# Weight sums moved to GpSimd in the third dense stage, and fraction bits to ScalarE in the last one

## The chip, the cores and the metric

One core of a Trainium2 chip runs the kernel: TensorE (matmuls), VectorE, ScalarE, GpSimd and the DMA queues, each with an in-order queue of its own. The metric is the time of one execution on the device in microseconds; of several runs the median counts.

## The reference, cut to what matters

Attention with a capped score feeds two feed-forward blocks. All dense weights arrive as 64-bit floats.

```
x = attention(q, k, v, cap)          # 2 x 12 heads, 448 tokens, 64 wide -> 896 x 768
h = x @ w_in1;  g = h * cos(h);      y = g @ w_out1     # 768 -> 2048 -> 768
h = y @ w_in2;  g = h * sigmoid(h);  out = g @ w_out2   # 768 -> 2048 -> 768
```

## The kernel before

**Stages.** The attention goes over twelve pairs of heads. Four dense stages follow: `gemm_in` (w_in1 and the cosine), `gemm_out` (w_out1), `gemm_sums` (w_in2 and the silu) and `gemm_last` (w_out2). Each engine works through its instructions in the order in which the program issues them; that order is written out by hand.

**Weights.** A block of 128 x 768 weights comes by DMA into `wraw` (two buffers) as pairs of 32-bit words, low word first. `w_abs` (line 135, ScalarE) turns the high word without its sign into a number with the exponent of a 32-bit float. `w_bits` then runs three VectorE operations, called conversions below: line 146 keeps the sign, line 148 shifts and adds the sign, line 151 adds the top three bits of the low word, the last three fraction bits. A pair of blocks has six conversions. The 32-bit result lies in `wx`. For the matmuls it is split into a high part, a rounded copy by ScalarE (`w_hi`, `take`, lines 159 and 709), and a low part, the difference, by VectorE (`w_lo`, `low`, lines 166 and 713); three matmuls (high x high, high x low, low x high) make a product exact enough.

**Third dense stage.** `gemm_sums` computes two output blocks from two weight blocks (a pair) and both batches by seven products M1 to M7 instead of eight, with sums of weight blocks. A product is nine matmuls. There are eight pairs, p = 0 to 7. The sums lie in one tile, `sums` in the trace: `s31` (line 689, 768 elements per partition) gives S31 and `s24` (lines 693 and 694, 384 each, the second from the first) gives S24. `A` and `A22` are blocks of the weights themselves. While TensorE works on pair p, the generator `weights(p+1)` issues the work on the next pair in seven portions: first block's conversions; second block's; `take` A and `s31`; `low` A and `take` S31; `s24` and `low` S31; `take` and `low` of S24; `take` and `low` of A22. Portions and products alternate. `copy` (line 789, ScalarE), `add` (line 761, VectorE) and `silu` (line 756, ScalarE) read the banks of the products:

```
m1(p)                      # bank A[p % 3]
c12(p - 1)                 # an add, line 761
next(w); m5_(p); next(w)   # the six conversions of pair p + 1
m7(p - 1)                  # add(p - 1 + HP, A[(p - 1) % 3], ...), line 761
next(w); m2(p); next(w); m6(p); next(w); next(w)
m4(p - 1)                  # goes on adding into bank A[(p - 1) % 3]
next(w); m3(p)
```

So `m4(p-1)` may start only when the `add` of `m7(p-1)` has read the bank, and that `add` is issued after the six conversions of pair p+1. In the round p = 1 there is no `m7(p-1)`, and `m4(0)` stands in its place.

**Last stage.** `gemm_last` has two halves of the output columns with eight weight blocks each and seven groups of 128 tokens; a weight block takes 42 matmuls. `last_w` prepares block n three blocks ahead: load, conversions, `w_hi`, `w_lo`, `w_abs` of the next. `g_split` (lines 934 and 935) splits the activations of the blocks p and p+8 in the same way, two rounds ahead.

Of the kernel before, what the change touches and what calls it, by code (L numbers as in the profile page):

```python
# [29 lines left out]
F32R = mybir.dt.float32r  # L30
I32 = mybir.dt.int32
U32 = mybir.dt.uint32
AF = mybir.ActivationFunctionType
ALU = mybir.AluOpType
PSUM = bass.MemoryType.PSUM
# [2 lines left out]
def tile_attention_ffn_ffn(  # L38
# [10 lines left out]
    nc = tc.nc  # L49
# [13 lines left out]
    HK = KD // 2  # L63
# [35 lines left out]
    wjobs = []  # L99
    for w_in, w_out in ((w_in1, w_out1), (w_in2, w_out2)):  # L100
        wi, wo = w_in.bitcast(I32), w_out.bitcast(I32)
        for n in range(KF):
            fc = n if w_out is w_out1 else n // 2 + n % 2 * HP
            wjobs.append((KD, wi[fc]))
        if w_out is w_out1:
            for dm in range(KD):
                for k0, k1 in cuts:
                    wjobs.append((k1 - k0, wo[dm][:, 2 * P * k0:2 * P * k1]))
        else:
            for half in range(DM // DH):  # L110
                for k0 in range(0, KF, KO):
                    wjobs.append((KO * DH // P, wo[half][:, 2 * DH * k0:2 * DH * (k0 + KO)]))
    wraw, w32, wlo, whi, loaded, guarded = {}, {}, {}, {}, set(), set()
    wx = wpool.tile([P, 2, KMAX, P], I32, name="wx")
    room = [wpool.tile([P, KMAX, P], F32R, name=f"hl{n}") for n in range(2 * NW)]
# [13 lines left out]
    def w_abs(i, t=None):  # L129
        if i not in wraw or i in guarded:  # L130
            return
        n = wjobs[i][0]
        guarded.add(i)
        w32[i] = wx[:, i % 2] if t is None else t
        nc.scalar.activation(out=w32[i][:, :n, :].bitcast(F32), in_=wraw[i][:, :n, :, 1].bitcast(F32), func=AF.Abs, scale=2.0 ** -112)  # L135

    def w_bits(i, step):
        if i >= len(wjobs):
            return
        n = wjobs[i][0]  # L140
        w1, w0 = wraw[i][:, :n, :, 1], wraw[i][:, :n, :, 0]
        if step == 0:
            w_abs(i)
        t = w32[i][:, :n, :]
        if step == 0:
            nc.vector.tensor_scalar(out=w1, in0=w1, scalar1=-0x80000000, scalar2=None, op0=ALU.bitwise_and)  # L146
        elif step == 1:
            nc.vector.scalar_tensor_tensor(out=t, in0=t, scalar=3, in1=w1, op0=ALU.logical_shift_left, op1=ALU.bitwise_or)  # L148
        else:
            t = t.bitcast(U32)  # L150
            nc.vector.scalar_tensor_tensor(out=t, in0=w0.bitcast(U32), scalar=29, in1=t, op0=ALU.logical_shift_right, op1=ALU.bitwise_or)  # L151
            del wraw[i]

    def w_hi(i):
# [3 lines left out]
        whi[i] = room.pop(0)  # L158
        nc.scalar.activation(out=whi[i][:, :n, :], in_=w32[i][:, :n, :].bitcast(F32), func=AF.Copy)  # L159

# [12 lines left out]
    with ExitStack() as actx:  # L173
# [19 lines left out]
        def v_init():  # L193
            nc.gpsimd.memset(ones[:, :2 * Q], 1.0)
            nc.gpsimd.memset(ones[:, 2 * Q:], 0.0)
# [53 lines left out]
        def S_tanh(p, t):  # L249
# [4 lines left out]
            n = 2 if t < 3 else 1  # L254
            nc.scalar.activation(out=e32[p][:, 2 * t:2 * t + n, :], in_=sc.pop((p, t))[:, :n, :S], func=AF.Tanh, scale=scap)  # L255

        def S_exp(p, chunks=slice(0, NCH)):
            if p >= NPT:
                return
            e = e32[p][:, chunks, :]  # L260
            nc.scalar.activation(out=e, in_=e, func=AF.Exp, scale=capt)  # L261

# [91 lines left out]
        for w, turn in ((0, 1), (1, 4), (2, 6)):  # L354
            for at, *step in ((0, w_abs, w), (1, w_bits, w, 0), (2, w_bits, w, 1), (3, w_bits, w, 2),
                              (3, w_load, w + 2, nc.gpsimd), (4, w_hi, w), (5, w_lo, w)):
                early.setdefault(turn + at, []).append(step)
        early.setdefault(NPT - 2, []).append((w_abs, 3))

        load(0)  # L360
        nc.vector.memset(zero.bitcast(F32), 0.0)
        warm_up(8, ps_o.tile([P, 512], F32, tag="sm", name="warm0")[:, :S])

        nc.scalar.activation(out=scap, in_=zero[:, :1].bitcast(F32), func=AF.Tanh)
        v_init()
# [128 lines left out]
    def w_do(f, ws, *a):  # L494
        for wi in ws:
            f(wi, *a)
# [5 lines left out]
    def cos_unit(pieces, ws):  # L502
        pieces = cut(pieces)
        for h, r, gh, gl in pieces:
            nc.scalar.activation(out=r.bitcast(I32), in_=h, func=AF.Copy, scale=1.0 / (2.0 * math.pi))
        w_do(w_bits, ws, 0)
        for h, r, gh, gl in pieces:
            nc.vector.scalar_tensor_tensor(out=r, in0=h, scalar=1.0 / (2.0 * math.pi), in1=r.bitcast(I32),
                                           op0=ALU.mult, op1=ALU.subtract)
        for h, r, gh, gl in pieces:  # L510
            nc.scalar.activation(out=r, in_=r, func=AF.Sin, scale=math.pi)
        w_next(ws)
        for h, r, gh, gl in pieces:
            nc.scalar.activation(out=r, in_=r, func=AF.Square)
        w_do(w_bits, ws, 1)
        w_do(w_bits, ws, 2)
        w_do(w_hi, ws)
        rest()
        for h, r, gh, gl in pieces:
            nc.vector.scalar_tensor_tensor(out=r, in0=r, scalar=-0.5, in1=h, op0=ALU.add, op1=ALU.mult)  # L520
        w_do(w_lo, ws)
        for h, r, gh, gl in pieces:
            nc.scalar.activation(out=gh, in_=r, func=AF.Copy)
            left.append((r, gh, gl))
# [142 lines left out]
    blocks, whole, xw = {}, {}, {0: wx}  # L667
# [18 lines left out]

    def s31(p):
        x = xw[p % 2].bitcast(F32)
        nc.vector.tensor_tensor(out=xw["s"][:, 0:2], in0=x[:, :, :HK, :], in1=x[:, 1].rearrange("p (n k) f -> p n k f", n=2), op=ALU.subtract)

    def s24(p):
        x, s = xw[p % 2].bitcast(F32), xw["s"]
        nc.vector.tensor_tensor(out=s[:, 2], in0=x[:, 0, :HK], in1=s[:, 1], op=ALU.subtract)
        nc.vector.tensor_tensor(out=s[:, 3], in0=x[:, 0, HK:], in1=s[:, 2], op=ALU.subtract)

    def source(p, what):
        x, s = xw[p % 2].bitcast(F32), xw["s"]
# [20 lines left out]
    def first_pair(n):  # L718
        if n == 0:
            w_half(0, 0)  # L720
        elif n == 1:
            s31(0)
            take(0, "A")
            low(0, "A")
            take(0, "S31")
            s24(0)
            low(0, "S31")
        else:
            take(0, "S24")
            low(0, "S24")  # L730
            take(0, "A22")
            low(0, "A22")
# [15 lines left out]
    def gemm_sums(pt0):  # L748
# [49 lines left out]
        def weights(q):  # L798
            w_load(base_s + 2 * q + 1)
            w_half(q, 0)  # L800
            w_load(base_s + 2 * q + 2)
            w_abs(base_s + 2 * q + 1, xw[q % 2][:, 1])
            yield
            w_half(q, 1)
            w_load(base_s + 2 * q + 3)
            yield
            take(q, "A")
            s31(q)
            yield
            low(q, "A")  # L810
            take(q, "S31")
            yield
            s24(q)
            low(q, "S31")
            yield
            take(q, "S24")
            low(q, "S24")
            yield
            take(q, "A22")
            low(q, "A22")  # L820
            abs_pair(q + 1)
            yield
# [237 lines left out]
```

## Time and profile before

| what | value |
|---|---|
| median of 3 runs | 551.69 us (551.6 to 552.08) |
| profiled execution | 551.79 us, of it 550.0 us span |
| granted TensorE clock, mean | 0.999 |
| TensorE busy | 542.1 us, 99% of the span |
| VectorE busy | 404.9 us, 74% |
| ScalarE busy | 309.0 us, 56% |
| GpSimd busy | 31.1 us, 6% |
| third dense stage, 327.29 to 429.44 us | VectorE 88.55 us busy, ScalarE 63.51, GpSimd 0 |
| last stage, 429.44 to 545.94 us | VectorE 64.56 us busy, ScalarE 38.15, GpSimd 0 |

The span is the stretch from the first to the last recorded instruction; the profiled execution's own time is somewhat longer. Busy time is work in the engine, not proof that the engine sets the end: the chain that ended last and the waits tell that.

### The profile page before, as it was taken

To read this page: it belongs to the slowest core of one execution; us is meant where nothing else is said; L and a number is where in the kernel's file an instruction comes from. 1 tells how busy PE (TensorE), PEld (TensorE's weight loads), DVE (VectorE), ACT (ScalarE), POOL (GpSimd) and SP (SyncE) were. 2 spreads that over 40 slices of the span, in tenths; PEclk is the share of its full clock that TensorE was granted. 3 is DMA by queue.
4 is the path that set the end of the run, shared out by engine and by line. 5 is a ranking of instruction groups with operands and counts; after the bars stand their busy time and mean duration, and the time that the engine had idled before them with its cause. 6 is when DMAs were issued, how large, how long until landed. Compare 5 with 4: busy or idle time off the path is not lost.

```text
span 550.0 us, 7421 instructions
## 1 busy us (share of the span) xinstructions
PE 542.1 (99%) x2940; PEld 467.2 (85%) x2940; DVE 404.9 (74%) x556; ACT 309.0 (56%) x393; POOL 31.1 (6%) x50
## 2 busy tenths in 40 slices
PE   8999999999999999999999999999999999999997
PEld 5444443999999999999999999999999999999996
DVE  4479997699888888666447888999886789537401
ACT  6989995477777665452323356566665556223101
POOL 0244432000000000000000000000000000000000
PEclk9999999999999999999999999999999999999999
DMA  7156652143322333452223603444331335164002
GB/s 291 55 141 199 171 166 78 44 142 120 109 94 102 115 95 106 153 154 88 72 99 103 217 8 114 147 160 153 116 114 58 116 116 172 58 215 144 30 1 101
DMA packets 17191, 65.13 MB, mean 118 GB/s; under 512 B 3384, under 2 KB 7268, under 8 KB 17156
## 3 DMA queue, kind: packets, MB, share of 16 engines
q1 hardware_dynamic: 14096, 54.94, 30.8%
q0 software_dynamic: 2496, 9.18, 5.4%
q10 hardware_dynamic: 564, 0.54, 0.3%
q8 instruction: 23, 0.38, 0.3%
q14 instruction: 12, 0.10, 0.1%
HBM read 61.74 MB, written 2.80 MB: 117 GB/s over the span
## 4 chain that ended last, share of the span: by engine, by line
PE 95%; ACT 2%; issue 1%; DMA 1%; DVE 1%
PE bank L473 21%; PE ps L473 21%; PE bank L967 21%; PE bank L741 19%; PE po L277 5%; PE sc L243 3%; PE sm L295 2%; PE sc L247 2%; PE po L287 2%; ACT e L255 1%; DMA raw<-in_qkv 1%; ACT e L261 1%; DVE e L303 0%; DVE ql L227 0%; DVE qh L226 0%
## 5 line engine op out<-in xcount | busy, mean ns | idle before, releaser
L473 PE MATMUL ps<-x,hl 128*128 128x448 f32 x576 | 117.0, 365 | 0.0
L473 PEld LDWEIGHTS ps<-x,hl 128*128 128x128 f32 x576 | 108.1, 188 | 9.2 <-DVE xs L314 0.7
L473 PE MATMUL bank<-gh,hl 128*128 128x448 f32 x288 | 83.9, 366 | 0.0
L159 ACT ACTIVATE hl<-wx 128x768 fp32r<-128x768 f32 (+1 forms) x44 | 35.8, 814 | 64.3 <-DVE wx L151 61.5
L967 PE MATMUL bank<-hl,gsh 128*128 128x384 f32 x280 | 71.0, 334 | 0.0
L151 DVE SCALAR_TENSOR_TENSOR wx<-wraw,wx 128x768 uint32<-128x768 uint32 (+1 forms) x66 | 61.6, 934 | 2.2
L148 DVE SCALAR_TENSOR_TENSOR wx<-wx,wraw 128x768 int32<-128x768 int32 (+1 forms) x66 | 61.5, 932 | 1.6
L135 ACT ACTIVATE wx<-wraw 128x768 f32<-128x768 f32 (+1 forms) x66 | 57.9, 877 | 6.3 <-DMA wraw<-in_moe_w_out 3.5
L473 PEld LDWEIGHTS bank<-gh,hl 128*128 128x128 f32 x288 | 54.1, 188 | 4.4
L166 DVE TENSOR_TENSOR hl<-wx,hl 128x768 fp32r<-128x768 f32 (+1 forms) x44 | 40.4, 918 | 20.4 <-ACT hl L159 20.3
L473 PE MATMUL bank<-gl,hl 128*128 128x448 f32 x144 | 52.6, 365 | 0.0
L967 PEld LDWEIGHTS bank<-hl,gsh 128*128 128x128 f32 x280 | 50.5, 188 | 0.0
L741 PE MATMUL bank<-T,hl 128*128 128x448 f32 x234 | 50.2, 365 | 0.0
L741 PEld LDWEIGHTS bank<-T,hl 128*128 128x128 f32 x234 | 43.9, 188 | 3.5
L967 PE MATMUL bank<-hl,gsl 128*128 128x384 f32 x140 | 46.8, 334 | 0.0
L255 ACT ACTIVATE e<-sc,scap 128x896 f32<-128x896 f32 (+1 forms) x48 | 40.0, 911 | 6.5 <-PE sc L243 6.5
L146 DVE TENSOR_SCALAR wraw<-wraw 128x768 int32<-128x768 int32 (+1 forms) x66 | 36.0, 546 | 5.1 <-ACT wx L135 4.9
L261 ACT ACTIVATE e<-e,capt 128x3136 f32<-128x3136 f32 (+2 forms) x13 | 35.2, 2710 | 0.4
L473 PE MATMUL bank<-g,hl 128*128 128x448 f32 x144 | 31.2, 365 | 0.0
L1000 DVE COPY os<-bank 128x384 f32<-128x384 f32 x6 | 3.3, 557 | 36.4 <-PE bank L967 36.4
L277 PE MATMUL po<-e,vf 128*64 128x448 f32 x144 | 29.4, 540 | 0.7 <-ACT e L261 0.7
L473 PEld LDWEIGHTS bank<-g,hl 128*128 128x128 f32 x144 | 27.1, 188 | 2.2
(107 smaller groups left out, 820.7 us busy)
## 6 DMA issues: line engine op xcount, KB each, us to landing
wraw<-in_moe_w_in SPq DMA_DIRECT2D x29, 768.0 KB, 4.2
wraw<-in_moe_w_out SPq DMA_DIRECT2D x22, 768.0 KB, 4.3
wraw<-in_moe_w_out SPq DMA_DIRECT2D x12, 640.0 KB, 4.1
raw<-in_qkv POOLq DMA_DIRECT2D x9, 480.0 KB, 4.6
out<-os SPq DMA_DIRECT2D x13, 192.0 KB, 1.9
rb<-rs SPq DMA_DIRECT2D x22, 112.0 KB, 3.3
wraw<-in_moe_w_in POOLq DMA_DIRECT2D x3, 768.0 KB, 6.4
vf<-in_qkv POOLq DMA_DIRECT2D x10, 224.0 KB, 4.6
```

The source lines that it names most:

```text
L135: nc.scalar.activation(out=w32[i][:, :n, :].bitcast(F32), in_=wraw[i][:, :n, :, 1].bitcast(F32), func=AF.Abs, scale=2.0 ** -112)
L146: nc.vector.tensor_scalar(out=w1, in0=w1, scalar1=-0x80000000, scalar2=None, op0=ALU.bitwise_and)
L148: nc.vector.scalar_tensor_tensor(out=t, in0=t, scalar=3, in1=w1, op0=ALU.logical_shift_left, op1=ALU.bitwise_or)
L151: nc.vector.scalar_tensor_tensor(out=t, in0=w0.bitcast(U32), scalar=29, in1=t, op0=ALU.logical_shift_right, op1=ALU.bitwise_or)
L159: nc.scalar.activation(out=whi[i][:, :n, :], in_=w32[i][:, :n, :].bitcast(F32), func=AF.Copy)
L166: nc.vector.tensor_tensor(out=wlo[i][:, :n, :], in0=w32.pop(i)[:, :n, :].bitcast(F32), in1=whi[i][:, :n, :].bitcast(F32), op=ALU.subtract)
L255: nc.scalar.activation(out=e32[p][:, 2 * t:2 * t + n, :], in_=sc.pop((p, t))[:, :n, :S], func=AF.Tanh, scale=scap)
L261: nc.scalar.activation(out=e, in_=e, func=AF.Exp, scale=capt)
L277: nc.tensor.matmul(po[u * D:(u + 1) * D], vf[p][:, 2 * t + u, :], e32[p][:, 2 * t + u, :], start=first and n == 0, stop=last and n == len( ...
L473: nc.tensor.matmul(pt, l, r, start=first and m == 0, stop=last and m == len(ops) - 1)
L741: nc.tensor.matmul(bank, x, y, start=first and m == 0, stop=m == len(ops) - 1, skip_group_check=True)
L967: nc.tensor.matmul(pt[t], a, r[:, cols], start=p == 0 and x == 0 and m == 0, stop=p == HP - 1 and x == 1 and m == 2)
```

## The change

Two edits. In the third dense stage the sums `s31` and `s24` are issued on GpSimd instead of VectorE for the pairs p = 2 to 7. In the last stage, for the last thirteen of its sixteen weight blocks, ScalarE reads the top byte of each low word, scales and shifts it so that the conversion to a whole number leaves its top three bits, and writes that whole number back as the low word, right behind `w_abs`. VectorE's three operations become two: the sign joined with the low word, then the shift joined with the result.

```
+    BYTES = len(wjobs) - 13
@@ w_abs
+        if i >= BYTES:
+            b = wraw[i][:, :n].rearrange("p k f t -> p (k f) t")
+            nc.scalar.activation(out=b[:, :, 0], in_=b.bitcast(U8)[:, :, 3], func=AF.Copy, scale=1.0 / 32, bias=-0.5 + 1.0 / 64)
@@ w_bits
-        if step == 0:
+        if i >= BYTES:
+            if step == 1:
+                nc.vector.scalar_tensor_tensor(out=w1, in0=w1, scalar=-0x80000000, in1=w0, op0=ALU.bitwise_and, op1=ALU.bitwise_or)
+            elif step == 2:
+                nc.vector.scalar_tensor_tensor(out=t, in0=t, scalar=3, in1=w1, op0=ALU.logical_shift_left, op1=ALU.bitwise_or)
+                del wraw[i]
+        elif step == 0:
@@ s31
-        nc.vector.tensor_tensor(out=xw["s"][:, 0:2], in0=x[:, :, :HK, :], in1=x[:, 1].rearrange("p (n k) f -> p n k f", n=2), op=ALU.subtract)
+        eng = nc.gpsimd if p > 1 else nc.vector
+        eng.tensor_tensor(out=xw["s"][:, 0:2], in0=x[:, :, :HK, :], in1=x[:, 1].rearrange("p (n k) f -> p n k f", n=2), op=ALU.subtract)
@@ s24
-        nc.vector.tensor_tensor(out=s[:, 2], in0=x[:, 0, :HK], in1=s[:, 1], op=ALU.subtract)
-        nc.vector.tensor_tensor(out=s[:, 3], in0=x[:, 0, HK:], in1=s[:, 2], op=ALU.subtract)
+        eng = nc.gpsimd if p > 1 else nc.vector
+        eng.tensor_tensor(out=s[:, 2], in0=x[:, 0, :HK], in1=s[:, 1], op=ALU.subtract)
+        eng.tensor_tensor(out=s[:, 3], in0=x[:, 0, HK:], in1=s[:, 2], op=ALU.subtract)
```

## Rows read from the trace of the kernel before

**Rows 1.** The page's chain that ended last, by engine.

```profile
PE 95%; ACT 2%; issue 1%; DMA 1%; DVE 1%
```

**Rows 2.** The same chain in order of time: start us, us, what.

```profile
327.29 102.15 PE bank L741 x504
429.44 116.50 PE bank L967 x672
```

**Rows 3.** Timeline of ScalarE, end of the last stage: start us, us, instruction, [idle before].

```profile
539.72 0.49 ACT L998 ACTIVATE os<-bank 128x384 f32<-128x384 f32 x1 [23.82 <-PE bank L967]
541.80 0.49 ACT L998 ACTIVATE os<-bank 128x384 f32<-128x384 f32 x1 [1.59 <-PE bank L967]
```

**Rows 4.** Timeline of VectorE, pair 2 of the third stage and what follows.

```profile
345.67 0.96 DVE L151 SCALAR_TENSOR_TENSOR wx<-wraw,wx 128x768 uint32<-128x768 uint32 x1
346.66 0.96 DVE L689 TENSOR_TENSOR sums<-wx 128x768 f32<-128x768 f32 x1
347.54 0.95 DVE L713 TENSOR_TENSOR hlx<-wx,hlx 128x768 fp32r<-128x768 f32 x1
348.41 0.55 DVE L693 TENSOR_TENSOR sums<-wx,sums 128x384 f32<-128x384 f32 x1
348.99 0.56 DVE L694 TENSOR_TENSOR sums<-wx,sums 128x384 f32<-128x384 f32 x1
...
352.34 0.55 DVE L146 TENSOR_SCALAR wraw<-wraw 128x768 int32<-128x768 int32 x1
...
357.26 0.62 DVE L761 TENSOR_TENSOR gf<-bank,m 128x448 f32<-128x448 f32 x1
...
369.05 0.62 DVE L761 TENSOR_TENSOR gf<-bank,m 128x448 f32<-128x448 f32 x1
```

**Rows 5.** Timeline of ScalarE in the same stretch.

```profile
347.65 0.85 ACT L709 ACTIVATE hl<-sums 128x768 fp32r<-128x768 f32 x1 [1.54 <-DVE sums L689]
...
357.91 0.58 ACT L756 ACTIVATE gf<-gf 128x448 f32<-128x448 f32 x1 [3.60 <-DVE gf L761]
358.40 0.83 ACT L709 ACTIVATE hl<-wx 128x768 fp32r<-128x768 f32 x1
```

**Rows 6.** Timeline of TensorE in the same stretch, neighbours of one kind merged.

```profile
350.84 3.81 PE L741 MATMUL bank<-T,hl 128*128 128x448 f32 x18
...
358.14 1.98 PE L741 MATMUL bank<-T,hl 128*128 128x448 f32 x9
```

**Rows 7.** Groups by line, GpSimd: count, busy us, mean ns of one, idle before.

```profile
L194 POOL MEMSET ones<- 128x64 f32 x1 | 0.2, 151 | 0.3 <-POOLq L1020 0.3
L195 POOL MEMSET ones<- 128x32 f32 x1 | 0.1, 125 | 0.0
```

**Rows 8.** Timeline of GpSimd in the attention stage, two stretches.

```profile
26.05 1.73 POOL L316 DMA_DIRECT2D sums<-xs  x2 [5.21 <-DVE sums L322]
...
28.35 0.93 POOL L215 DMA_DIRECT2D vf<-in_qkv  x1
...
82.34 1.22 POOL L316 DMA_DIRECT2D sums<-xs  x2 [2.21 <-DVE sums L322]
```

**Rows 9.** Timeline of VectorE in the same stretches.

```profile
27.06 0.57 DVE L226 CAST qh<-raw 128x832 fp32r<-128x832 f32 x1
...
28.60 0.56 DVE L146 TENSOR_SCALAR wraw<-wraw 128x768 int32<-128x768 int32 x1
...
82.41 1.02 DVE L303 TENSOR_TENSOR e<-e 128x896 f32<-128x896 f32 x1
```

**Rows 10.** Groups by line, ScalarE, last stage alone.

```profile
L135 ACT ACTIVATE wx<-wraw 128x768 f32<-128x768 f32 x14 | 12.5, 893 | 3.5 <-DMA wraw<-in_moe_w_out 3.5
```

**Rows 11.** Timeline of VectorE, first round of the last stage.

```profile
436.85 2.09 DVE L935 TENSOR_TENSOR gsl<-gf,gsh 128x896 fp32r<-128x896 f32 x2 [0.68 <-ACT gsh L934]
```

**Rows 12.** Timeline of TensorE, third round of the last stage.

```profile
443.84 0.51 PE L967 MATMUL bank<-hlx,gsh 128*128 128x384 f32 x2
```

More of the change, by code (lines that the diff above doesn't have):

```diff
@@ L32 @@
 U32 = mybir.dt.uint32
+U8 = mybir.dt.uint8
 AF = mybir.ActivationFunctionType
```

## The prediction

> **What bounds the kernel now.** I read the chain that ended last first, then its pieces in order of time, then the waits, then the timelines around the two edits. TensorE holds 95% of the chain [rows 1]. The third dense stage is one unbroken piece: 504 matmuls in 102.15 us, 202.7 ns each; the last stage is another: 672 in 116.50 us, 173.4 ns each [rows 2]. The waits name nobody for TensorE in either. So there is nothing to win in them unless a matmul itself gets cheaper when VectorE works less. Late in the last stage, with the weights done and VectorE idle, 12 matmuls still lie between two evacuations 2.08 us apart, 173.3 ns each [rows 3]: the same. The edits can move work about under a bound engine; the question is whether they uncover it.
>
> They could. The thinnest cover of the third stage is seen by following one pair through the queues. While TensorE multiplies pair p, VectorE makes the blocks of pair p+1, in order: six conversions, the sums, the four low parts, and, between them, additions (line 761) that read TensorE's banks. One addition matters: `add` of `m7(p-1)` stands behind the six conversions of pair p+1, and the product `m4(p-1)` accumulates into the very bank that it reads. In the round p=2 it runs from 357.26 to 357.88 us [rows 4], and `m4(1)` starts at 358.14 [rows 6]. The cover is 0.26 us. VectorE's round takes 11.79 us from that addition to the next (357.26 to 369.05), TensorE's 12.77 (seven products of 102.15 / 56 = 1.824 us), so later the cover grows by about a microsecond a round; this first place decides.
>
> **Sums on GpSimd: the price of one.** From pair 2 on (six pairs) `s31` and the two halves of `s24` leave VectorE: 0.96 + 0.55 + 0.56 us of it per pair [rows 4]. GpSimd shows no two-input operation in this trace, only memsets: 151 ns for 64 elements, 125 for 32 [rows 7], that is 0.81 ns an element and 0.10 fixed. One such pass over 768 elements gives 0.72 us (0.41 for 384) and is the lower bound. Two reads and a write, each a pass, one after the other give 1.97 (1.03): the upper bound. If the write runs beside the reads, two passes give 1.35 (0.72). I take the middle of the last two, 1.66 (0.88), as a two-input operation is nearer to reading twice than to writing once.
>
> The Trainium skill (GPSIMD Engine Reference, Elementwise — side-by-side cycle accounting) gives about 2.6 cycles an element for a two-input operation; at its 1.2 GHz I estimate 1.66 us for 768 from that, by which the sum would be the same. No run here shows it yet.
>
> **Do the two engines exclude each other?** In the attention stage GpSimd issues DMAs of about 0.6 us. Two of them take 1.22 us at 82.34, beside a two-input addition of VectorE, but 1.73 at 26.05, where a CAST at double rate (832 elements in 0.57 us) follows: the second ends at 27.78, 0.15 after the CAST's end at 27.63. Another takes 0.93 us and ends at 29.28, 0.12 after a one-input operation of the same rate that ends at 29.16 [rows 8, 9]. So GpSimd waits for a whole VectorE instruction of some forms, and goes on some 0.1 us after it. Beside two-input ones an issue isn't held, but it only writes. A double-rate one-input operation and a two-input one read alike (832 in 0.57 us; twice 896 in 1.02): if reads are what collide, a GpSimd subtraction, which reads, will collide with both forms. I take it that it does, in either direction, with 0.1 us at each hand-over.
>
> The Trainium skill (SBUF — State Buffer, SBUF: two separate sides) says that VectorE and GpSimd share one pair of ports, that whichever starts first holds it for the whole instruction, and that VectorE needs it in its double-rate forms and, against a GpSimd operation that reads, with two SBUF inputs. By this rule the sum is 556.0 us; by the row of the two-input addition alone, which held up no issue, it is 552.1. The trace agrees for the double-rate forms (0.15 and 0.12 us after their ends) and cannot show the other.
>
> **The sum, pair 2.** Handing over to another engine costs 0.03 us (347.62 to 347.65), an instruction that waits for nothing starts 0.08 before its forerunner's end [rows 4, 5]. Conversions end at 346.63. VectorE is first, as its next instruction needs no signal: the low part of A, 346.66 to 347.62. `s31` on GpSimd 347.72 to 349.38. ScalarE takes S31 to 350.26 (0.85 [rows 5]); the first half of `s24` 349.41 to 350.29; low part of S31 350.32 to 351.27; the second half of `s24` 351.37 to 352.25; take S24 to 353.13; low part of S24 353.16 to 354.12; low part of A22 to 354.59, addition to 355.13. The next six conversions start at 355.04 instead of 352.34, take 4.92 us as before, and the addition that `m4(1)` needs ends at 360.58. `m4(1)` starts at 360.61 instead of 358.14: **2.47 us lost**. `m5(2)`, due at 350.84 [rows 6], waits some 0.2 us on the way, inside that figure.
>
> **The later pairs.** From that addition (359.96): ScalarE's silu after it 0.58, take A 0.83 [rows 5], to 361.94; meanwhile `s31` 359.99 to 361.65 and half of `s24` to 362.56, which holds the low part of A until 362.66; low A and low S31 to 364.50; second half of `s24` to 365.48; take S24 366.36; low S24 367.35; low A22, addition, conversions from 368.27; next addition at 373.19. A round of 13.23 us against TensorE's 12.77 loses 0.46, in four more rounds (`m4(2)` to `m4(5)`) 1.84. What VectorE was spared, 2.07 us a pair, it now waits in the low parts, and the conversions and the bank's addition are queued behind them. GpSimd's own queue holds nothing else by then.
>
> **Fraction bits on ScalarE.** Thirteen of the last stage's sixteen blocks lose VectorE's 0.55 us operation (line 146; 13 x 0.55 = 7.2 us) and get a ScalarE copy from bytes to whole words with the shape and stride of line 135, 0.89 us [rows 10]: 13 x 0.89 = 11.6 us. The two remaining VectorE operations keep their form. Bounds: 0.49, what ScalarE needs for half the elements [rows 3], and twice 0.89 for the byte access; I take 0.89, the same stride. Behind it in ScalarE's queue stand the splits of the activations; the tightest, for blocks 2 and 10, is done on VectorE at 438.94 [rows 11] and needed at 443.84 [rows 12]. One copy ahead makes it 0.9 later (1.8 at the upper bound), of 4.9. TensorE covers this edit: nothing. Uncovered, a copy would cost at most itself.
>
> **Sum:** the profiled execution took 551.79 us (span 550.0, 1.79 around it); 551.79 + 2.47 + 1.84 = 556.1. The median of the runs is 0.10 below that execution, so 556.0. GpSimd at 1.97 and 1.03 adds 0.61 both to the loss of pair 2 and to each round: 4.3 + 5 x 0.61 = 7.4, so 559.1. At two passes pair 2 loses 2.47 - 0.63 = 1.84 and later rounds nothing: 553.5. At one pass 0.6: 552.3.
>
> **Rivals.** A measurement of this kernel can tell 0.2%, 1.1 us, from no change.
> 1. No exclusion: for it, the issue beside the two-input addition [rows 8, 9]. Then `s31` starts at 346.68, both halves of `s24` end at 350.16, the addition ends at 358.49, `m4(1)` starts 0.38 late, and later rounds of 11.2 us stay below TensorE's. 552.1; with the upper price of GpSimd 552.7. This is the case on the other side: not slower. It decides as long as a pair's detour adds less than 0.26 + 1.1 us.
> 2. A cheap subtraction near one pass, with exclusion: 552.3, no change.
> 3. GpSimd dearer than three passes, 2.5 and 1.3: 4.15 for pair 2 and a round of 14.9 us, 4 x 2.15 more: 564.4. No row speaks against it but the memsets.
> 4. Faster: some hidden dependence of TensorE on VectorE that the freed time removes. Against it: no wait and equal spacing beside an idle VectorE [rows 2, 3]. At the most the 0.1 us of scatter, or a per cent of the stage, 550.7.
> 5. ScalarE's copies late: needs over 4.9 us at once; 552 to 553. The edit does its work but frees nothing that counts.
>
> **Chances.** Forecast with exclusion, 553.5 to 559.2: 0.55. Rival 1: 0.24 (0.02 of it slower). Rival 2: 0.05. Rival 3: 0.12. Faster: 0.03. Rival 5: 0.01. Slower: 0.55 + 0.02 + 0.12 + 0.01 = 0.70; same: 0.22 + 0.05 = 0.27; faster 0.03. The range reaches from no change, 551.5, to a little above the upper price, 560.0; it leaves out most of rivals 3 and 4.
>
> **What would show it.** The third stage's piece of matmuls grows from 102.15 to about 106.5 us, the last stage stays at 116.5; TensorE's weight loads wait for line 761, first before `m4(1)` near 358 us. Low parts (line 713) that start while GpSimd subtracts last longer than 0.96 us, or GpSimd's spans stretch beside them. If the price of GpSimd is near 1.7 us and nothing stretches, rival 1 holds. Waits of TensorE in the last stage would prove the step on the fraction bits wrong, and a first wait elsewhere than at `m4(1)` the reading of the cover.

## The result and the profile after

The changed kernel takes 558.23 us (median of 4 runs, 557.99 to 558.76) against 551.85 for the kernel before on the same chip: a ratio of 1.0117, 95% interval 1.0099 to 1.0135. It is 6.4 us slower. The profiled execution took 558.08 us, 556.3 of it span.

The chain that ended last no longer belongs to TensorE alone ([rows 1] had PE at 95%, DVE at 1%):

```profile
PE 82%; DVE 7%; POOL 4%; ACT 4%; issue 3%; POOLq 0%; DVEq 0%
```

The third and the last stage by windows: stretch, its length, busy time of TensorE, its weight loads, VectorE, ScalarE and GpSimd, then the granted clock, the DMA share and GB/s:

```profile
327.29:435.90 108.61, 105.72 (x504) 95.20 (x503) 79.15 (x101) 62.08 (x104) 30.69 (x18) 0.98 0.36 116
435.90:552.40 116.50, 116.50 (x673) 116.35 (x671) 58.31 (x65) 49.05 (x64) 0.00 (x0) 1.00 0.31 102
```

The third stage has grown from 102.15 us to 108.92 (from 327.15, 0.14 earlier than in [rows 2], to 436.07 by the chain in order of time); the last stage has kept its 116.5. After the last matmul the span ends 3.7 us later instead of 4.0, so that the whole is 6.4 longer and not 6.8. All of the loss is in the stage with the sums. GpSimd is busy there for 30.7 us with 18 subtractions, and VectorE for 79.15 us instead of 88.55.

TensorE's timeline around the first loss, to be held against [rows 6]:

```profile
356.35 1.98 PE L754 MATMUL bank<-T,hlx 128*128 128x448 f32 x9
360.22 3.36 PE L754 MATMUL bank<-T,hl 128*128 128x448 f32 x9 [1.88 <-DVE gf L774]
363.37 2.34 PE L754 MATMUL bank<-B,hlx 128*128 128x448 f32 x9
365.55 2.02 PE L754 MATMUL bank<-B,hl 128*128 128x448 f32 x9
367.41 3.88 PE L754 MATMUL bank<-T,hl 128*128 128x448 f32 x18
```

`m4(1)` starts at 360.22 instead of 358.14 and waits for line 774, the addition that was line 761. The next product starts 3.15 us later, though nine matmuls used to take 1.82: that is the clock, told below. VectorE in the same stretch:

```profile
346.41 0.95 DVE L726 TENSOR_TENSOR hlx<-wx,hlx 128x768 fp32r<-128x768 f32 x1
349.98 0.99 DVE L726 TENSOR_TENSOR hl<-sums,hl 128x768 fp32r<-128x768 f32 x1 [2.61 <-ACT hl L722]
352.75 0.96 DVE L726 TENSOR_TENSOR hlx<-sums,hlx 128x768 fp32r<-128x768 f32 x1 [1.78 <-PE bank L754]
...
359.54 0.62 DVE L774 TENSOR_TENSOR gf<-bank,m 128x448 f32<-128x448 f32 x1
361.54 0.96 DVE L726 TENSOR_TENSOR hl<-wx,hl 128x768 fp32r<-128x768 f32 x1 [1.38 <-ACT hl L722]
362.70 1.48 DVE L726 TENSOR_TENSOR hl<-sums,hl 128x768 fp32r<-128x768 f32 x1 [0.20 <-ACT hl L722]
...
372.77 0.62 DVE L774 TENSOR_TENSOR gf<-bank,m 128x448 f32<-128x448 f32 x1
```

And GpSimd:

```profile
346.67 2.39 POOL L701 TENSOR_TENSOR sums<-wx 128x768 f32<-128x768 f32 x1 [256.73 <-DVE wx L162]
349.14 1.01 POOL L706 TENSOR_TENSOR sums<-wx,sums 128x384 f32<-128x384 f32 x1
350.23 1.61 POOL L707 TENSOR_TENSOR sums<-wx,sums 128x384 f32<-128x384 f32 x1
359.77 1.83 POOL L701 TENSOR_TENSOR sums<-wx 128x768 f32<-128x768 f32 x1 [7.93 <-DVE wx L162]
361.69 1.68 POOL L706 TENSOR_TENSOR sums<-wx,sums 128x384 f32<-128x384 f32 x1
363.44 1.61 POOL L707 TENSOR_TENSOR sums<-wx,sums 128x384 f32<-128x384 f32 x1
```

Line 726 is the low part (713 before), 701, 706 and 707 are the sums. Read the two fences together. `s31` of pair 2 spans 2.39 us because the low part of A runs until 347.36: from there it takes 1.70. In pair 3, where VectorE's only neighbour is the addition out of a bank, it spans 1.83. The first half of `s24` spans 1.01 us when it has the field to itself (349.14) and 1.68 behind the low part of A (361.54 to 362.50, then 0.87). The low part of S31 spans 1.48 instead of 0.96 when it comes upon that half. From one addition to the next VectorE's round is 372.77 - 359.54 = 13.23 us; in the kernel before it was 11.79 [rows 4].

In the last stage ScalarE's new copies cost what was expected, and no instruction of TensorE waits:

```profile
L140 ACT ACTIVATE wraw<-wraw 128x768 int32<-128x768 uint8 x13 | 11.6, 891 | 0.0
```

### The profile page after: what moved, and what is told of

Read it like the earlier page. It is cut to its first block, busy times and chain, and to the rows that moved or that the text cites. A ratio compares the mean times of both kernels' runs of the same rounds, so it can differ in the third digit from the quotient of the medians.

```text
span 556.3 us, 7440 instructions
## 1 busy us (share of the span) xinstructions
PE 545.9 (98%) x2940; PEld 467.8 (84%) x2940; DVE 389.2 (70%) x525; ACT 318.7 (57%) x406; POOL 62.1 (11%) x68
## 4 chain that ended last, share of the span: by engine, by line
PE 82%; DVE 7%; POOL 4%; ACT 4%; issue 3%; POOLq 0%; DVEq 0%
PE bank L484 21%; PE ps L484 21%; PE bank L980 21%; PE bank L754 5%; PE po L288 4%; PE sc L254 4%; DVE wx L159 2%; PE sm L306 2%; POOL sums L701 2%; PE sc L258 2%; PE po L298 2%; POOL sums L706 2%; ACT e L266 1%; DVE wx L162 1%; POOL sums L707 1%
## 5 line engine op out<-in xcount | busy, mean ns | idle before, releaser
L754 PE MATMUL bank<-T,hl 128*128 128x448 f32 x234 | 52.7, 375 | 2.9 <-DVE gf L774 2.7
L162 DVE SCALAR_TENSOR_TENSOR wx<-wraw,wx 128x768 uint32<-128x768 uint32 (+1 forms) x53 | 49.2, 928 | 1.7
L159 DVE SCALAR_TENSOR_TENSOR wx<-wx,wraw 128x768 int32<-128x768 int32 (+1 forms) x53 | 49.0, 925 | 1.1
L701 POOL TENSOR_TENSOR sums<-wx 128x768 f32<-128x768 f32 x6 | 11.7, 1942 | 296.4 <-DVE wx L162 296.4
L754 PE MATMUL bank<-B,hlx 128*128 128x448 f32 x129 | 29.7, 371 | 0.0
```

The lines of the kernel that those rows point to most:

```text
L701: eng.tensor_tensor(out=xw["s"][:, 0:2], in0=x[:, :, :HK, :], in1=x[:, 1].rearrange("p (n k) f -> p n k f", n=2), op=ALU.subtract)
L754: nc.tensor.matmul(bank, x, y, start=first and m == 0, stop=m == len(ops) - 1, skip_group_check=True)
```

## The experiments

Theory: GpSimd and VectorE shut each other out, a pair's detour over GpSimd makes VectorE's round 13.2 us long, and the additions that TensorE's banks need come late. Rivals: the long spans are simply the price of a subtraction on GpSimd; the loss is that of the one thin cover ahead of `m4(1)`; TensorE's clock makes part of it.

**e1: the fraction bits alone.**

```diff
-        eng = nc.gpsimd if p > 1 else nc.vector
+        eng = nc.vector
```

> The sums stay on VectorE, only the thirteen byte copies are made by ScalarE. Theory (TensorE covers this edit): the last stage stays at 116.5 us, ScalarE's copy takes 0.89 us each, VectorE does 7.2 us less, the time is that of before within 0.2%, 551.1 to 552.6. Rival (the copies stand in ScalarE's queue ahead of the splits and hold up TensorE): TensorE waits in the last stage, 552.6 or more.

Measured: 551.37 us against 551.73, ratio 0.9993 (0.9984 to 1.0002). Both stages keep their 102.15 and 116.50 us, ScalarE's copy takes 0.892 us, VectorE is busy 58.00 us in the last stage instead of 64.56. The edit moves 6.6 us of work off VectorE (7.2 expected) and nothing in the time.

**e2: only `s31` on GpSimd** (`s24` back to `nc.vector`).

> Byte copies as in the changed kernel; of the sums only s31 (768 elements) goes to GpSimd, s24 stays on VectorE. Exclusion (a GpSimd subtraction costs 1.7 us and the two engines shut each other out): s31 runs about 2.4 us behind the low part of A in pair 2, TensorE loses 0.9 us once and the rounds stay below 12.77 us: about 552.7. Own price (the long spans are what a subtraction costs, nobody is shut out, 1.9 us): 0.3 lost, 552.1. Either way the bulk of the 6.4 us must be missing; if 2 us or more are left, the reading of the rounds is wrong.

Measured: 552.40 us against 551.73, ratio 1.0014 (1.0005 to 1.0023). The loss of 0.7 lies between the two expectations, 0.9 and 0.3, too near to both to decide by the time. GpSimd's spans of pairs 2 and 3 say more:

```profile
346.70 2.39 POOL L701 TENSOR_TENSOR sums<-wx 128x768 f32<-128x768 f32 x1 [256.73 <-DVE wx L162]
358.22 1.84 POOL L701 TENSOR_TENSOR sums<-wx 128x768 f32<-128x768 f32 x1 [9.13 <-DVE wx L162]
```

In pair 2 the low part of A runs beside it until 347.39 (0.95 from 346.44), and the subtraction is done 1.70 us after that; in pair 3, without such a neighbour, it takes 1.84, and in the last four 1.84 or 1.85. The executions fall into two groups: seven took 552.08 to 552.59 us, the profiled one (552.11) among them, and four 553.46 to 553.49, at a mean granted clock of 0.999 or 1.000 in both groups. What the four lost is not shown. The run does show that `s31` alone makes little of the 6.4 us.

**e3: only `s24` on GpSimd** (`s31` back to `nc.vector`).

> Byte copies as in the changed kernel; only the two halves of s24 go to GpSimd, s31 stays on VectorE. Exclusion: low S31 comes between the halves, the addition ahead of m4(1) is some 1.7 us late, a round takes about 12.9 us and the last additions are late again: 4.8 us lost, 556.6. Own price (two halves of 1.6 us beside VectorE): 2.8 lost, 554.6. No effect of either: 551.9.

Measured: 552.81 us against 551.73, ratio 1.0018 (1.0009 to 1.0027). Both numbers missed. TensorE waits once, ahead of `m4(1)`, where two products start 3.11 us apart instead of 1.82 (1.29 lost), and never again, since a round takes 370.75 - 358.71 = 12.04 us and not 12.9. GpSimd first, then VectorE, show why:

```profile
347.75 1.57 POOL L706 TENSOR_TENSOR sums<-wx,sums 128x384 f32<-128x384 f32 x1 [257.74 <-DVE sums L701]
...
360.34 1.02 POOL L706 TENSOR_TENSOR sums<-wx,sums 128x384 f32<-128x384 f32 x1 [9.34 <-DVE sums L701]
361.43 1.61 POOL L707 TENSOR_TENSOR sums<-wx,sums 128x384 f32<-128x384 f32 x1
```

```profile
358.71 0.62 DVE L774 TENSOR_TENSOR gf<-bank,m 128x448 f32<-128x448 f32 x1
...
360.71 1.46 DVE L726 TENSOR_TENSOR hl<-wx,hl 128x768 fp32r<-128x768 f32 x1 [0.51 <-ACT hl L722]
362.09 1.77 DVE L726 TENSOR_TENSOR hl<-sums,hl 128x768 fp32r<-128x768 f32 x1
...
370.75 0.62 DVE L774 TENSOR_TENSOR gf<-bank,m 128x448 f32<-128x448 f32 x1
```

I had let VectorE run two low parts in a row before GpSimd's second half. The engines take turns instead: the first half (until 361.36) holds up the low part of A, which ends at 362.17; then the second half goes (0.87 us, to 363.04), and the low part of S31 waits for it, 1.77 us in all. The half that GpSimd has to itself is 1.02 us long, one that finds VectorE at work 1.57 to 1.61: a price of its own would not change with the neighbour. Neither sum alone makes the loss: by itself each costs 0.7 or 1.1 us, as VectorE's round stays below TensorE's 12.77, at 11.79 in e2 (additions at 358.00 and 369.79) and 12.04 here. Together they bring it to 13.23.

**e9: both engines side by side, with no data between them.** To the kernel before, in the first round of the last stage:

```diff
+ for x in range(24):
+     nc.gpsimd.tensor_tensor(out=idle[:, :KD * P], in0=src[:, :KD * P], in1=src[:, P:KD * P + P], op=ALU.subtract)
```

> The kernel before, with 24 subtractions of 768 elements added on GpSimd in the last stage, whose result nobody reads; they begin about 437 us and wait for nothing, while VectorE runs its conversions, splits and, from about 475 us, nothing. Exclusion: alone a subtraction takes about 1.7 us; beside VectorE spans on both sides lengthen, by up to a whole instruction of the other (GpSimd 1.7 to 2.7, VectorE's 0.96 us forms to 1.5 or more). Own price: GpSimd takes the same 1.9 us with and without VectorE, and VectorE's forms keep 0.96 and 0.56 us.

Measured, in one run: 580.88 us against 552.13. VectorE's timeline while GpSimd subtracts (until some 497 us), and after:

```profile
440.88 2.19 DVE L146 TENSOR_SCALAR wraw<-wraw 128x768 int32<-128x768 int32 x1
443.11 2.48 DVE L148 SCALAR_TENSOR_TENSOR wx<-wx,wraw 128x768 int32<-128x768 int32 x1
445.63 2.48 DVE L151 SCALAR_TENSOR_TENSOR wx<-wraw,wx 128x768 uint32<-128x768 uint32 x1
...
497.33 0.96 DVE L148 SCALAR_TENSOR_TENSOR wx<-wx,wraw 128x768 int32<-128x768 int32 x1
...
502.07 0.56 DVE L146 TENSOR_SCALAR wraw<-wraw 128x768 int32<-128x768 int32 x1
```

GpSimd's group by line: count, busy us, mean ns.

```profile
L977 POOL TENSOR_TENSOR idle<-gsh 128x768 f32<-128x768 f32 x24 | 57.8, 2409 | 348.7 <-ACT gsh L934 346.9
```

The 0.96 us forms with two inputs become 2.48, the one-input double-rate form 0.56 becomes 2.19: each grows by 1.5 to 1.6 us, most of one subtraction, until the subtractions end. They take turns one instruction each: from 437.2 to 497.3 us 24 subtractions and 25 VectorE instructions run. TensorE waits 24.3 us for the splits, though no result of GpSimd is read by anyone; the rest of the 28.8 us is not taken apart, and the granted clock was 0.84 in that stretch. Exclusion is shown, for both forms and in both directions. The Trainium skill (SBUF — State Buffer, SBUF: two separate sides) has the rule: VectorE in its double-rate forms, or with two SBUF inputs against a GpSimd operation that reads, holds a port pair that GpSimd needs, for a whole instruction. The trace agrees, with 2.48 for 0.96 and 2.19 for 0.56.

**e8: the sums alone** (`BYTES = len(wjobs)`).

> Sums on GpSimd as in the changed kernel, fraction bits as before. If the fraction bits cost and bring nothing: 558.2. If they hide part of the loss or add to it, it differs by over 0.2%.

Measured: 558.88 us against 551.83, ratio 1.0126 (1.0111 to 1.0141): the loss is there without the fraction bits, and the intervals of this and the changed kernel overlap. In the profiled execution the granted clock stayed at 1.00, so its timeline of TensorE shows the waits alone:

```profile
356.92 1.98 PE L754 MATMUL bank<-T,hlx 128*128 128x448 f32 x9
360.79 2.10 PE L754 MATMUL bank<-T,hl 128*128 128x448 f32 x9 [1.88 <-DVE gf L774]
...
371.84 1.98 PE L754 MATMUL bank<-T,hlx 128*128 128x448 f32 x9
374.02 2.12 PE L754 MATMUL bank<-T,hl 128*128 128x448 f32 x9 [0.20 <-DVE gf L774]
...
424.76 1.98 PE L754 MATMUL bank<-T,hl 128*128 128x448 f32 x9
427.56 2.09 PE L754 MATMUL bank<-T,hl 128*128 128x448 f32 x9 [0.82 <-DVE gf L774]
429.87 2.09 PE L754 MATMUL bank<-T,hl 128*128 128x448 f32 x9 [0.23 <-ACT m L802]
431.80 1.98 PE L754 MATMUL bank<-B,hl 128*128 128x448 f32 x9
434.56 2.09 PE L754 MATMUL bank<-T,hl 128*128 128x448 f32 x9 [0.78 <-DVE gf L774]
```

A product takes 1.82 us from start to start. Ahead of `m4(1)` it is 3.87: 2.05 lost. From `m4(1)` to `m4(2)` it is 13.23 us, VectorE's round to the hundredth, 0.46 over TensorE's own 12.77. And then the last pair: 2.80, 2.31 and 2.76 us between starts, 0.98 + 0.49 + 0.94 = 2.4 lost, ahead of `m4(6)`, behind it, and ahead of `m4(7)`. By the chain in order of time the stage is 108.93 us long: 2.22 more than before up to `m4(1)` (33.07 from the stage's start against 30.85), four rounds of 0.46, and 2.7 from `m4(5)` on. That is 0.3 more than the 2.4, some 0.1 us in each product that follows a wait (the one at 429.87 takes 1.93 to the next start).

**e4: sums on GpSimd from pair 5 on** (`p > 4`).

> The changed kernel with the sums on GpSimd from pair 5 on only (three pairs instead of six), where VectorE has gained some 2 us on TensorE. Theory (a round of VectorE of 13.2 us is longer than TensorE's 12.77, and VectorE must be ahead at the last additions of pair 7): the lead is eaten up and about 2.2 us are lost at the end of the stage, 554.0. Rival (what counts is the one thin cover ahead of m4(1), 0.26 us; later the cover is 2 us): nothing is lost, 551.9.

Measured: 553.03 us against 551.73, ratio 1.0022 (1.0014 to 1.0031). The 1.3 us lost lie nowhere near `m4(1)`: TensorE does not wait before 421 us, in pair 7. In rounds of 13.23 us (additions at 380.77, 394.00 and 407.22) VectorE's lead shrinks: ahead of `m4(5)` it is 2.1 us in the kernel before (the addition ends at 407.08, the product starts at 409.21) and 1.2 here (407.84, 409.03); ahead of `m4(6)` it is down to 0.1 (421.69, 421.79). Behind `m4(6)` a copy and ahead of `m4(7)` an addition are then late, by 0.4 and 0.95 us. The rival of the one thin cover is out; my 2.2 was too much.

**e7: pair 7 back on VectorE** (`1 < p < HP - 1`).

> The changed kernel with the sums of pair 7 back on VectorE (pairs 2 to 6 on GpSimd). The last round of VectorE is shorter by some 1.4 us. If the additions of the last pair (chain of VectorE) set the end: 1.2 to 1.5 us come back, 556.9. If the waits ahead of m4(1) to m4(5) alone make the loss, as predicted: 558.2.

Measured: 556.77 us against 551.83, ratio 1.0090 (1.0077 to 1.0103); against e8 on the same chip 2.1 us come back, a little more than expected. The wait ahead of `m4(6)` is gone, the one ahead of `m4(7)` (0.95) stays, though this pair's sums are back on VectorE; the section on the prediction says why.

**e5: pair 2 alone on GpSimd** (`p == 2`).

> The changed kernel with the sums of pair 2 alone on GpSimd, so VectorE's later rounds are as before and nothing but the first wait is left. If that wait costs only itself (about 2.2 us ahead of m4(1)): 554.0. If, as the changed kernel's trace suggests, it also brings TensorE's clock down to 0.50 for some 3.5 us (1.7 us lost) and leaves matmuls 207 instead of 203 ns apart for 300 of them (1.2 us): 2.2 + 1.7 + 1.2 = 5.1, so 556.8, and the stage then ends by TensorE, not by VectorE.

Measured: 555.63 us against 551.83, ratio 1.0062 (1.0048 to 1.0077), scattered more than any other kernel: 553.56 and 554.26 in the two executions whose mean granted clock was 0.999 and 1.000, 555.63, 555.63, 555.72 and 556.89 in the four at 0.996. The profiled execution is one of the latter; its windows show why (columns as above, the clock third from the right):

```profile
358.40:360.60 2.20, 0.34 (x2) 0.00 (x0) 2.17 (x4) 0.00 (x0) 0.00 (x0) 1.00 0.88 254
...
361.80:365.00 3.20, 3.20 (x10) 2.86 (x9) 2.91 (x5) 2.65 (x6) 0.00 (x0) 0.50 0.53 215
```

TensorE stood still for some 2 us, worked for one more, and then was granted 0.50, the 1.2 GHz level, for 3.2 us: ten matmuls where 15.8 of 0.203 us fit, 1.2 us lost in that window alone. Here TensorE sets the end (the chain runs over its 351 matmuls from `m4(1)` to the last stage without another engine), and the fall of the clock costs about 1.8 us in the executions that have it: 555.7, the middle of the four, against 553.9, the mean of the two. My 5.1 held the wider spacing too, which did not come.

**e6: the wait ahead of `m4(1)` filled with ten idle matmuls.**

```diff
+ for x in range(10):
+     nc.tensor.matmul(bank[1][:, :S], h[:, 0], T["T2", 0].view()[:, 0, :], start=True, stop=True, skip_group_check=True)
```

> The changed kernel with ten idle matmuls (2.03 us, into a bank that nobody reads) put where TensorE waits ahead of m4(1). If the low clock and the wider spacing were on the path that sets the end, they go and about 2.9 us come back: 555.3. If the chain of VectorE, ScalarE and GpSimd sets the end of the stage, TensorE only waits later and longer for the same additions: 558.2, unchanged within 1 us, with the clock at 1.00 and 203 ns spacing.

Measured: 558.53 us against 551.83, ratio 1.0125 (1.0112 to 1.0138). The clock stays up, the spacing stays at 203 ns, and not a microsecond comes back: TensorE reaches the additions sooner and waits there longer. In the changed kernel the clock is off the path that sets the end. The executions say the same: it took 557.99 us at a mean clock of 1.000 and 558.08, 558.38 and 558.76 at 0.996 or 0.997; e8 took 559.03 and 559.16 at 1.000 and 558.47 and 558.72 at 0.996.

## Why the prediction was right, and where it fell short

**What bounds the kernel: right.** Moving work off VectorE and not stalling TensorE brings nothing (e1).

**The thin cover ahead of `m4(1)`: right in place and size.** Forecast 2.47 us lost; measured 2.22, in the changed kernel (360.22 - 358.14, and 0.14 for the earlier start) as in e8.

**The price of a subtraction: right.** Forecast 1.66 and 0.88 us; measured 1.70 behind a hold-up and 1.83 without, 0.87 behind one and 1.01 without. The forecast was the middle between two bounds from memsets, a choice that no row then decided.

**Exclusion: right**, and shown by e9 without any dependence of data. Rival 1 (no exclusion, 552.1) is out. The order of the turns was partly wrong: I had the low part of A wait for the first half of `s24`; in pair 3 it came first, and the half waited. VectorE's round came out at 13.23 us all the same, forecast and measured, so part of that agreement is luck; in e3 the same slip cost the expectation.

**The sum: one term too small.** The step that failed is "loses 0.46, in four more rounds (`m4(2)` to `m4(5)`) 1.84", with nothing behind it, and ahead of it "later the cover grows by about a microsecond a round; this first place decides". The 0.46 is there in e8. But I stopped counting at `m4(5)`. In pair 7 three more additions and copies stand behind the last sums, and the trace of the kernel before could have told that its cover does not last. VectorE's additions ahead of `m4(6)` and `m4(7)`, and TensorE (`m4(6)` is the second of the three products that start at 420.15, at 421.97; `m4(7)` starts at 427.45):

```profile
418.89 0.62 DVE L761 TENSOR_TENSOR gf<-bank,m 128x448 f32<-128x448 f32 x1
...
426.25 0.62 DVE L761 TENSOR_TENSOR gf<-bank,m 128x448 f32<-128x448 f32 x1
```

```profile
420.15 5.63 PE L741 MATMUL bank<-T,hl 128*128 128x448 f32 x27
425.63 1.99 PE L741 MATMUL bank<-B,hl 128*128 128x448 f32 x9
427.45 1.99 PE L741 MATMUL bank<-T,hl 128*128 128x448 f32 x9
```

The cover is 2.46 us ahead of `m4(6)` and only 0.58 ahead of `m4(7)`. The same two additions in e8:

```profile
426.89 0.62 DVE L774 TENSOR_TENSOR gf<-bank,m 128x448 f32<-128x448 f32 x1
...
433.89 0.62 DVE L774 TENSOR_TENSOR gf<-bank,m 128x448 f32<-128x448 f32 x1
```

They lie 7.00 us apart, in e4 and e7 as well: between them the chain of e8 goes through silus and a split of the activations on ScalarE, and through the low parts of two splits and three conversions of the last stage on VectorE. TensorE needs 5.47 us for the three products from `m4(6)` to `m4(7)`, so VectorE has to be some 1.5 us ahead at `m4(6)`; with the sums on GpSimd it was not, and in e7 the lead there is back to some 0.5 us only (addition until 425.73, product at 426.24). From `m4(5)` on e8 loses 2.7 us; e4 and e7 put loss there too. 2.22 + 1.84 + 2.7 = 6.8, the growth of the stage. With that term the forecast of 556.0 would have been 558.7, against 558.23. The measured time lies inside the stated range, but the range had its room above 556.0 for a dearer subtraction, and the subtraction cost what was forecast: that the missing term fitted into that room is luck.

**The fraction bits: right** (e1: nothing; the copy 0.892 us there and 0.891 in the changed kernel, forecast 0.89).

**Not foreseen:** the clock. It would have been a mistake to add it: it falls in three of the changed kernel's four executions, and in e6 and e8 the loss is the same without it.

## What to carry to other kernels

Before moving work to an idle engine, ask what the two engines share: here GpSimd's and VectorE's instructions took turns, so 2.07 us a pair off VectorE came back as waiting. Follow a lengthened round to the last consumer of the stage, not to the last place where it repeats, and read the cover at each of them: a lead that another engine has built up is spent there. And before pricing a slow clock or a widened gap, see which engine sets the end: an engine that then only waits longer loses nothing by it.

## What the runs showed of the hardware

- GpSimd and VectorE alternate one instruction each when both have work (e9: 24 subtractions, mean span 2.41 us, beside 25 VectorE instructions, with 2.4 to 2.5 us for its conversions of 0.96).
- The same wait of some 2 us brought TensorE's granted clock to 0.50 in some executions of a kernel and not in others: in e5 the mean clock was 0.996 in four of six, in e8 in two of four, and e8's profiled execution lost 2.05 us ahead of `m4(1)` and kept 1.00. In the changed kernel's profile:

```profile
358.20:360.20 2.00, 0.13 (x1) 0.00 (x0) 1.93 (x3) 0.01 (x1) 0.43 (x1) 1.00 0.84 270
...
361.20:362.20 1.00, 1.00 (x4) 0.92 (x3) 0.66 (x1) 1.00 (x3) 0.92 (x2) 0.50 0.66 233
```

- After that episode the changed kernel's matmuls lay 1.86 us per product apart (365.55 to 367.41 above) instead of 1.82, at a granted clock of 1.00, until the next wait near 427 us. In e5 the spacing returned to 1.82 after a like episode. What makes the difference stays open.
